# Block-sparse attention and a gated feed-forward in one kernel: mask rows by ScalarE, more zero products at the start, a spread mean product, V casts on VectorE, and a reordered end

## The chip, the cores and the metric

The kernel runs on one core of a Trainium2 chip. A core has five engines with a queue each: TensorE for matrix products (PE in the profile, with its weight loads as PEld), VectorE (DVE), ScalarE (ACT), GpSimd (POOL) and SyncE (SP), which here only issues DMAs. Each engine works through its instructions in order; they wait for one another by semaphores. The metric is the device time of one launch in microseconds (us). Before the change the median of three runs is 231.93 us, from 230.8 to 233.28.

## The reference

Attention over four batches of eight heads, 768 positions and 64 channels per head, with a mask made of blocks of 32, and then a feed-forward layer over the 3072 tokens of 512 channels:

```python
scores = scale * q @ k.T                 # per batch and head
# allowed: neighbouring blocks, first and last block row and column,
# and three sampled blocks for each block of queries
scores = np.where(mask, scores, -1e9)
attn = exp(scores - max) / sum
x = (attn @ v), heads side by side       # 3072 x 512

h = x @ w_in                             # 3072 x 1024
solu = h * softmax(h)
ln = (solu - mean) / sqrt(var + 1e-6) * g_ln
out = ln @ w_out                         # 3072 x 512
```

## The kernel before

**Tiling.** A batch is cut into three passes of 256 queries, so there are 12 passes. A pass has 12 units: four pairs of heads, three units for a pair, each unit 256 keys of both heads by 256 queries. A unit is four score products into a PSUM tile `sco` (two buffers), one exponential of 128x1024 on ScalarE (`exps`), and eight products of the exponentials with V (`outs`) into the tile `op` (one buffer). After the third unit of a pair VectorE normalises `op` into `xb`. The mask is part of the score product: below the 64 channels, `KT` and `QT` hold 24 more rows, block selectors for the keys and mask values for the queries.

**Feed-forward.** It runs one pass behind, in two layers of 128 tokens: `xb` is turned by a DMA into `xT`, eight products with `w_in` give `h` (`h_mms`, one PSUM buffer), ScalarE takes its exponential (`e_exp`), VectorE multiplies (`solu`) and takes statistics, a DMA turns `solu` into `lnT`, eight products with the centred weights `w_cen_sb` give `o` (`o_mms`), and VectorE scales and a DMA stores. The division by the softmax sum and by the standard deviation is folded into one factor, which GpSimd computes (`rstd`). The centred weights are prepared once: GpSimd multiplies `w_out` by `g_ln` (`prep_w`), TensorE takes its mean over the layer (`prep_mean`, eight products), VectorE copies the mean and subtracts it (`prep_cen`, eight times).

**Order.** Everything is unrolled and put in order by hand: `at(when, fn, ...)` files a step under a due time in units, `emit()` sorts by it, and what is emitted in this order is queued on its engine in this order. Unit 144 is the `end`. Steps before the plan (the mask, the first casts and turns, `scores(0)` and `scores(1)`) are emitted as they stand in the text. `zeros(n, pool)` issues n products of a zero tile (128x512) whose result nobody reads.

**The places the change touches.** The first mask rows of q: ScalarE copies them for head 0 from `m_ps` (line 599), VectorE copies head 0 to head 1 (line 604); ScalarE also brings the first turned q chunk to `QT` (line 602). `turn` of pairs 2 and 3 (lines 627 to 633). `prep_mean` at 19.0 and 19.6 and `prep_cen` from 19.9 (lines 684 to 688). `coming` (line 703), which files loads and casts of the next batch, the casts on GpSimd. The end: the list from line 880, with the last pass's layers (`x_last`, `h_end`, `ln_mm`, `ln_out`, `o_half`, `scale_half`), and `check_e` and `check_bad`, which test that all sums lie in a safe range. TensorE adds up the flags (`bad_ps`), VectorE writes them as an integer (`bad_i`), and lines 926 and 927 load it on every engine and branch around a slow general path that these inputs do not need.

## Time and profile before

| | |
|---|---|
| median of three runs | 231.93 us (230.8 to 233.28) |
| the profiled execution, its own time | 230.46 us |
| its span, first to last instruction | 228.5 us |
| TensorE busy | 210.6 us of the span |
| ScalarE busy | 174.0 us |
| VectorE busy | 154.2 us |
| GpSimd busy | 111.4 us |
| mean granted TensorE clock | 0.98 |

The page gives busy time by engine, then the span in 40 slices, the DMA queues, the chain of work that ended last, and the costliest groups of instructions. A busy share is an average over the whole span: stages with different limits are told apart by windows and by the timeline. A line of the timeline has the start in us, the duration in us, engine, line, operation, output and input tile, shapes and count, and in brackets the idle time of the engine just before it with what ended it. A row with several instructions has the time from the first one's start to the last one's end; matmuls overlap, so a row of several is shorter than the sum. A window row has the window, its length, the busy time (and number of instructions) of PE, PEld, DVE, ACT and POOL, then the granted TensorE clock, the DMA share and GB/s. The profiled execution's own time is 1.96 us above its span, and 1.47 us below the median.

### The profile page before, as it was taken

The numbers are of one execution on the slowest core, as the hardware profiler recorded it, in microseconds if no ns is written. First come the engines' busy times: TensorE is split into PE (matmuls) and PEld (weight loads), VectorE is DVE, ScalarE is ACT, GpSimd is POOL, SyncE is SP. The second block draws the span as 40 slices with busy tenths as digits, with TensorE's granted clock in tenths as the row PEclk, the third lists the DMA queues.
The fourth block names the chain that finished last, engine by engine and source line by source line (L and its number), as shares of the span: only waits on it lengthen the run. The fifth ranks groups of instructions, "written<-read, shape, count | busy, mean of one in ns | idle before, by whom it ended". The sixth has DMA issues, their size and how long they took to land.

```text
span 228.5 us, 5931 instructions
## 1 busy us (share of the span) xinstructions
PE 210.6 (92%) x2368; PEld 146.4 (64%) x2368; DVE 154.2 (68%) x352; ACT 174.0 (76%) x205; POOL 111.4 (49%) x155
## 2 busy tenths in 40 slices
PE   7896997999989999999999999999999999996970
PEld 2565864776756777776866777677676767663440
DVE  7876666877775765676775676667657655765860
ACT  4667885797786988797798898779789888783730
POOL 7999965247897325647825507739600000000010
PEclk9679999999999999999999999999999999999998
DMA  6999593339979449839749569489233458434021
GB/s 192 362 324 268 149 283 133 73 72 339 290 87 314 99 86 289 241 64 299 155 30 351 129 147 246 114 165 296 52 98 92 87 54 117 115 89 87 37 101 56
DMA packets 56148, 37.60 MB, mean 165 GB/s; under 512 B 38068, under 2 KB 51636, under 8 KB 56116
## 3 DMA queue, kind: packets, MB, share of 16 engines
q1 hardware_dynamic: 55172, 35.60, 61.5%
q0 software_dynamic: 528, 1.05, 2.4%
q10 hardware_dynamic: 416, 0.52, 0.8%
q8 instruction: 20, 0.33, 0.6%
q14 instruction: 12, 0.10, 0.1%
HBM read 23.07 MB, written 6.29 MB: 129 GB/s over the span
## 4 chain that ended last, share of the span: by engine, by line
PE 75%; DVE 9%; POOL 7%; DMA 3%; issue 2%; ACT 1%; DVEq 0%; POOLq 0%
PE sco L364 24%; PE o L481 14%; PE h L421 14%; PE op L388 14%; PE tp_k L329 2%; POOL KT L309 2%; POOL QT L309 2%; PE tp_q L329 2%; PE he L789 2%; DMA xT<-xb 1%; PE warm L556 1%; DVE xb L402 1%; DMA xTe<-xb 1%; DVE KT L309 1%; DVE w_cen_sb L673 1%
## 5 line engine op out<-in xcount | busy, mean ns | idle before, releaser
L375 ACT ACTIVATE exs<-sco 128x1024 bf16<-128x1024 f32 x144 | 141.6, 1025 | 16.5 <-PE sco L364 13.8
L364 PE MATMUL sco<-QT,KT 88*128 88x256 bf16 x576 | 88.6, 275 | 3.1 <-ACT exs L375 1.6
L364 PEld LDWEIGHTS <-KT 88*128 88x128 bf16 x576 | 55.5, 98 | 34.5 <-issue 7.2
L421 PE MATMUL h<-w_in_sb,xT 128*128 128x512 bf16 x176 | 55.2, 378 | 1.2 <-DVE solu L442 0.6
L388 PE MATMUL op<-VA,exs 128*128 128x65 bf16 x1152 | 52.0, 194 | 2.6 <-DVE xb L402 1.7
L388 PEld LDWEIGHTS <-exs 128*128 128x128 bf16 x1152 | 48.8, 97 | 6.0 <-issue 2.6
L474 POOL TENSOR_TENSOR rstd<-vpe,mhalf 128x1 f32<-128x1 f32 x24 | 13.2, 549 | 71.5 <-DVE vpe L472 64.6
L481 PE MATMUL o<-w_cen_sb,lnT 128*128 128x512 bf16 x176 | 45.1, 379 | 0.0
L430 ACT ACTIVATE e<-h 128x1024 bf16<-128x1024 f32 x22 | 22.5, 1023 | 20.5 <-PE h L421 19.1
L309 POOL COPY KT<-pt_k 64x768 bf16<-64x768 bf16 x24 | 19.7, 822 | 23.5 <-DVE pt_k L338 22.8
L401 DVE RECIPROCAL recip_all<-op 128x4 f32<-128x4 f32 x48 | 8.7, 181 | 30.6 <-PE op L388 30.3
L456 DVE BATCH_NORM_STATS2 stats<-solu 128x6 f32<-128x512 bf16 x46 | 29.3, 680 | 0.0
L442 DVE TENSOR_TENSOR solu<-h,e 128x1024 bf16<-128x1024 f32 x22 | 26.7, 1214 | 1.2 <-ACT e L430 1.2
L481 PEld LDWEIGHTS <-lnT 128*128 128x128 bf16 x176 | 15.8, 97 | 13.3
L492 DVE TENSOR_SCALAR ot<-o,rstd 128x512 f32<-128x512 f32 x20 | 15.0, 751 | 11.2 <-issue 6.3
L402 DVE TENSOR_TENSOR xb<-op,recip_all 128x256 bf16<-128x256 f32 x48 | 20.4, 424 | 1.7
L309 POOL COPY QT<-pt_q 64x768 bf16<-64x768 bf16 x24 | 19.7, 820 | 3.6 <-DVE pt_q L338 2.3
L421 PEld LDWEIGHTS <-xT 128*128 128x128 bf16 x176 | 15.5, 98 | 5.9 <-DMA xT<-xb 1.6
L309 POOL CAST qn<-st_q 128x768 bf16<-128x768 f32 (+2 forms) x19 | 14.4, 763 | 1.8 <-DMA st_q<-in_q_dram 1.5
L309 POOL CAST kn<-st_k 128x768 bf16<-128x768 f32 x15 | 12.7, 845 | 4.4 <-DMA st_k<-in_k_dram 2.9
L309 POOL CAST VA<-st_v 128x768 bf16<-128x768 f32 x16 | 13.1, 834 | 1.5 <-DMA st_v<-in_v_dram 1.3
L338 DVE COPY pt_q<-tp_q 128x768 bf16<-128x768 bf16 x12 | 6.7, 556 | 10.3 <-PE tp_q L329 10.3
(92 smaller groups left out, 151.5 us busy)
## 6 DMA issues: line engine op xcount, KB each, us to landing
st_v<-in_v_dram SPq DMA_DIRECT2D x16, 384.0 KB, 5.6
out_dram<-ot SPq DMA_DIRECT2D x23, 256.0 KB, 3.6
st_k<-in_k_dram SPq DMA_DIRECT2D x15, 384.0 KB, 4.6
st_q<-in_q_dram SPq DMA_DIRECT2D x12, 384.0 KB, 4.8
w_out_f<-in_moe_w_out_dram SPq DMA_DIRECT2D x4, 512.0 KB, 8.5
st_q<-in_q_dram SPq DMA_DIRECT2D x4, 256.0 KB, 6.9
w_in_sb<-in_moe_w_in_dram POOLq DMA_DIRECT2D x1, 1024.0 KB, 12.9
st_q<-in_q_dram SPq DMA_DIRECT2D x4, 128.0 KB, 4.3
```

The source lines that it names most:

```text
L309: eng.tensor_copy(out=o, in_=i)
L364: nc.tensor.matmul(sco[:, hh, kk * QW : (kk + 1) * QW], KT[b % 2][0:KR, h * NCH + 2 * u + kk, :], QT[b % 2][0:KR, h * NCH + PC * j : h * N ...
L375: nc.scalar.activation(out=exs_of[ps, pr][:, u].rearrange("p a b c -> p (a b c)"), in_=sco_of.pop(s).rearrange("p a b -> p (a b)"), func=A ...
L388: nc.tensor.matmul(op[:, hh, ic, :], exs[:, u, hh, kk, ic * TQ : (ic + 1) * TQ], VA[b % 2][:, 2 * pr + hh, 2 * u + kk, :], start=(u == 0 a ...
L402: nc.vector.tensor_tensor(out=xb_of[ps][:, :, 2 * pr * D : 2 * (pr + 1) * D].rearrange("p c (h d) -> p h c d", h=2), in0=op[:, :, :, 0:D], ...
L421: nc.tensor.matmul(h_of[ps, i][:, half, :], xT_of[ps][:, i * KD + c, :], w_in_sb[:, c, half * HF : (half + 1) * HF], start=(c == 0), stop= ...
L430: nc.scalar.activation(out=o, in_=h, func=ACT.Exp, scale=1.0, accum_out=esum_all[:, t : t + 1])
L442: nc.vector.tensor_mul(out=so, in0=h, in1=e)
L456: nc.vector.bn_stats(out=stat_of[ps, i][:, half, :], in_=so[:, half, :])
L474: nc.gpsimd.tensor_tensor(out=rstd_of[ps, i], in0=vpe, in1=mhalf, op=ALU.pow)
L481: nc.tensor.matmul(ops_of[ps, i], lnT_of[ps, i][:, c, :], w_cen_sb[:, c, :], start=(c == 0), stop=(c == KF - 1), skip_group_check=True)
L492: nc.vector.tensor_scalar(out=o, in0=i_, scalar1=r, scalar2=None, op0=ALU.mult)
```

## The change

Six edits. (1) ScalarE copies the first mask rows of q to both heads from PSUM, and VectorE brings the first turned q chunk to `QT`. (2) The zero products ahead of the first scores go into one tile: one more before the k turn, three in place of one after the q turn; after each of the units 0 to 3 three stand in place of two. The q turn of pair 3 is due one unit later. (3) The mean of `w_out` is taken two products at a time, at 19.85, 20.85, 21.85 and 22.85, and the eight subtractions are due from 23.1 on. (4) For batch 1, V of pairs 1 to 3 is cast by VectorE at fixed times, and the last V load is filed with the one before it. (5) At the end the order of the list is new: five products of the last but one pass's first layer come before the end, the last chunk of x is turned ahead of all products of the last pass's h, and these follow in one run; products of the older layers are regrouped. (6) The test is split: `check_e` early, the sum (`check_sum`) after the last factors, and `check_bad` last, behind both halves of the last output; the second half is scaled by ScalarE.

```diff
         def zeros(n, pool=p_o):
-            w = pool.tile([128, 512] if pool is not p_sco else [128, 2, 512], FP32,
-                          tag={p_o: "o", p_op: "op", p_sco: "sco"}[pool], name="warm")
-            w = w[:, 0, :] if pool is p_sco else w
+            w = pool
+            if pool in (p_o, p_op):
+                w = pool.tile([128, 512], FP32, tag="o" if pool is p_o else "op", name="warm")
...
-        row_q0 = rows(QT[0], 0, 1).rearrange("p o (i c) -> p (o i) c", i=2)
         mask_rows(nc.gpsimd, KT[0], 2)
         mask_rows(nc.vector, KT[0], 0)
+        warm_t = p_sco.tile([128, 2, 512], FP32, tag="sco", name="warm_t")[:, 0, :]
+        zeros(1, warm_t)
         turn_mm(0, 0, "k", p_op, 2, NCH)
-        zeros(1, p_sco)
+        zeros(1, warm_t)
         turn_out(0, 0, "k", DVE2, 0, 2)
-        nc.scalar.copy(out=row_q0, in_=m_ps[D:KR, :, 0 : S // 2])
+        for hh in range(2):
+            nc.scalar.copy(
+                out=rows(QT[0], hh, hh + 1).rearrange("p o (i c) -> p (o i) c", i=2),
+                in_=m_ps[D:KR, :, 0 : S // 2])
         turn_mm(0, 0, "q", p_o, 0, 2)
-        zeros(1, p_sco)
-        turn_out(0, 0, "q", (nc.scalar, nc.scalar), 0, 2)
+        zeros(3, warm_t)
+        turn_out(0, 0, "q", DVE2, 0, 2)
         turn_out(0, 0, "k", DVE2, 2, NCH)
-        nc.vector.tensor_copy(out=rows(QT[0], 1, 2), in_=rows(QT[0], 0, 1))
...
-            turn(w0 + 0.05, 0, pr, "q", p_o, 0, 2)
+            turn(w0 + (0.05 if pr == 2 else 1.0), 0, pr, "q", p_o, 0, 2)
...
         for n in range(4):
-            at(n + 0.9, zeros, 2, p_op)
+            at(n + 0.9, zeros, 3, p_op)
...
-            at(19.9 + 0.4 * c, prep_cen, c)
-        at(19.0, prep_mean, 0, 4)
-        at(19.6, prep_mean, 4, KF)
+            at(23.1 + 0.45 * c, prep_cen, c)
+        for n in range(4):
+            at(19.85 + n, prep_mean, 2 * n, 2 * n + 2)
...
-                at(t0 + 8.2 + 1.2 * n, cast, nc.gpsimd, b, pr, key)
+                if b == 1 and key == "v" and pr > 0:
+                    at((0, 38.6, 40.2, 43.2)[pr], cast, nc.vector, b, pr, key)
+                else:
+                    at(t0 + 8.2 + 1.2 * n, cast, nc.gpsimd, b, pr, key)
...
-                n_ld = [0, 0, 4, 0, 6, 1, 1]
+                n_ld = [0, 0, 4, 0, 6, 2, 0]
...
-        def scale_half(half, eng):
+        def scale_half(half, eng, q):
...
+            if eng is nc.scalar:
+                nc.scalar.activation(out=ot_of[LP, 1][:, m0:m1], in_=o2[half], func=ACT.Copy,
+                                     scale=rstd_of[LP, 1])
...
         def check_e():
-            check_r(n_r - 2 * PC, n_r)
             in_range(okr[:, n_r:], esum_all, 1e-6, 1e7)
+
+        def check_sum():
             nc.vector.reduce_sum(out=n_ok[:, 0:1], in_=okr, axis=AX.X)
```

The list at the end, as it stands after the change (`A` is ScalarE, `V` VectorE, `LP` the last pass):

```python
(o_mms, LP - 1, 0, 5, 8), (scaled, LP - 1, 0, A), (store, LP - 1, 0),
(x_last,), (h_end, 0, 0, KD - 1), (h_end, 0, KD - 1, KD),
(stats, LP - 1, 1), (rstd, LP - 1, 1), (check_r, n_r - 2 * PC, n_r),
(e_exp, LP, 0), (h_end, 1, 0, KD), (solu, LP, 0), (e_exp, LP, 1),
(o_mms, LP - 1, 1, 0, 3, tile_in(p_op, "op", "o_10")),
(ln_mm, 0), (ln_out, 0, A), (o_mms, LP - 1, 1, 3, 8), (solu, LP, 1),
(check_e,), (stats, LP, 0), (squares, 1), (ln_mm, 1), (ln_out, 1, V),
(o_mms, LP, 0, 0, 8, tile_in(p_sco, "sco", "oe0")), (mean_mms, 1),
(scaled, LP - 1, 1, A), (store, LP - 1, 1), (rstd, LP, 0), (rstd_sq, 1),
(check_sum,), (scaled, LP, 0, A), (store, LP, 0),
(o_half, 0, p_sco, "sco"), (o_half, 1, p_op, "op"),
(scale_half, 0, V, nc.sync), (scale_half, 1, A, nc.scalar), (check_bad,)
...
at(end - 1.15, o_mms, LP - 1, 0, 0, 5)    # before: at(end - 1.1, h_end, 0, 0, KD - 1)
```

Before, this list began with `o_mms` of five products, `x_last`, `stats`, two more `o_mms` and the last chunk of `h_end`; `check_e` and `check_bad` stood between the factors and the second `o_half`.

35 lines of the change are left out of this document (17 added, 18 removed).

## The prediction

> **What bounds the kernel now.** I read the page first (busy time, slices, chain of waits), then windows to tell the stages apart, then the timeline of those stages in which TensorE idles or runs slowly.
>
> ```profile
> PE 210.6 (92%) x2368; PEld 146.4 (64%) x2368; DVE 154.2 (68%) x352; ACT 174.0 (76%) x205; POOL 111.4 (49%) x155
> ...
> PEclk9679999999999999999999999999999999999998
> ...
> PE 75%; DVE 9%; POOL 7%; DMA 3%; issue 2%; ACT 1%; DVEq 0%; POOLq 0%
> ```
>
> TensorE is busy 92% of the span and carries 75% of the chain. The slices 1 and 2 (5.7 to 17 us) have a clock of 0.6 and 0.7. The windows show where there is room:
>
> ```profile
> 4.50:7.91 3.41, 2.40 (x16) 0.95 (x14) 3.24 (x7) 2.54 (x6) 3.28 (x4) 1.00 1.06 347
> 7.91:11.32 3.41, 3.24 (x19) 2.49 (x20) 2.61 (x7) 2.08 (x3) 3.36 (x6) 0.50 1.07 364
> 11.32:14.74 3.42, 3.42 (x18) 2.13 (x17) 2.14 (x3) 2.01 (x2) 3.01 (x4) 0.50 1.08 359
> 205.87:209.28 3.41, 1.65 (x22) 1.03 (x22) 2.02 (x5) 2.03 (x3) 0.55 (x1) 1.00 0.30 63
> ...
> 38.00:46.00 8.00, 6.24 (x83) 4.76 (x82) 7.21 (x18) 6.02 (x9) 1.99 (x3) 1.00 0.32 61
> 72.00:80.00 8.00, 8.00 (x97) 5.72 (x96) 4.97 (x12) 6.92 (x8) 4.13 (x6) 1.00 0.59 175
> ```
>
> From 7.91 to 14.74 TensorE has half the clock and is busy all the time: there it is the bound because it is slow. From 72 on it is busy without a gap, and nothing in the change removes work there. From 38 to 46 it idles 1.76 of 8 us while VectorE is nearly full. So four places can give time: the start, the mean and its subtraction, the wait for V, and the end. Everything between follows the start of its stage, so a microsecond won early is carried along.
>
> **Part 1, the start.** The first score products wait for the mask row that VectorE copies last:
>
> ```profile
> 5.63 0.79 ACT L599 CAST QT<-m_ps 24x768 bf16<-24x768 f32 x1
> 5.64 1.50 DVE L309 COPY KT<-tp_k 64x256 bf16<-64x256 bf16 x4
> 7.16 0.86 DVE L604 COPY QT<-QT 24x768 bf16<-24x768 bf16 x1
> 8.08 0.61 PE L364 MATMUL sco<-QT,KT 88*128 88x256 bf16 x2 [0.84 <-DVE QT L604]
> 8.72 1.02 ACT L375 ACTIVATE exs<-sco 128x1024 bf16<-128x1024 f32 x1 [1.52 <-PE sco L364]
> ```
>
> After the change ScalarE makes both row copies, 5.63 + 0.79 + 0.79 = 7.21. VectorE brings two k pieces, then two of q, about 0.3 each, to 7.0. The five zero products there are hidden behind these copies. Scores start at 7.28 instead of 8.08, the first exponential at 7.9 instead of 8.72: 0.8 won. The larger share is the clock.
>
> ```profile
> 12.75 1.06 PE L556 MATMUL warm<-zer 128*128 128x512 bf16 x2
> 15.04 0.60 PE L556 MATMUL warm<-zer 128*128 128x512 bf16 x2
> 12.14 1.08 DVE L590 COPY QT<-QT 24x1536 bf16<-24x1536 bf16 x1
> 14.48 1.14 DVE L309 COPY KT<-tp_k 64x768 bf16<-64x768 bf16 x2 [1.26 <-PE tp_k L329]
> 15.23 2.86 ACT L375 ACTIVATE exs<-sco 128x1024 bf16<-128x1024 f32 x3 [1.22 <-PE sco L364]
> 18.95 0.59 DVE L309 COPY QT<-tp_q 64x256 bf16<-64x256 bf16 x2
> 20.36 0.66 PE L388 MATMUL op<-VA,exs 128*128 128x65 bf16 x16 [1.34 <-DVE xb L402]
> 21.56 1.94 ACT L375 ACTIVATE exs<-sco 128x1024 bf16<-128x1024 f32 x2 [1.25 <-PE sco L364]
> ```
>
> The clock changes 3.41 us apart, at 4.50, 7.91 and 14.74; it fell after a window with TensorE busy 2.40, some of it transposes, and it held at the end of the window at 205.87 with 1.65 and no transposes. The first of these windows gets three more zero products, some 0.65 at full clock, and the scores 0.8 earlier; I therefore take it that the clock holds. Then VectorE sets the pace: from 7.0 it has two more k pieces, the mask rows and the turned k and q of pairs 1 and 2. Walked with these rows (up to 1.08 for mask rows, 1.14 for a pair's k, 0.59 for its q) it brings pair 2 at 14.25, and the seventh exponential starts at 14.9; it is the third of the three at 15.23, so at 17.1 before (15.23 + 2.86 - 1.02): 2.2 won. The four zero products in the units 0 to 3 cost nothing, as TensorE has slack at full clock; with the clock still down they cost 0.43 each. The q turn of pair 3, one unit later, takes 0.59 of copies from in front of the normalisation for which TensorE waited 1.34 at 20.36. Together the tenth exponential, at 21.56 before, comes at 19.1 to 19.4. I take 2.4; bounds 0.6 (clock down) and 2.8.
>
> **Part 2, mean and centring.**
>
> ```profile
> 33.98 1.89 PE L667 MATMUL mean_ps<-w_out_sb,mean_w 128*128 128x512 bf16 x8
> 37.07 1.02 ACT L430 ACTIVATE e<-h 128x1024 bf16<-128x1024 f32 x1 [2.30 <-PE h L421]
> 39.15 0.60 PE L364 MATMUL sco<-QT,KT 88*128 88x256 bf16 x4 [1.43 <-ACT exs L375]
> 40.35 0.61 PE L421 MATMUL h<-w_in_sb,xT 128*128 128x512 bf16 x2 [0.61 <-DVE solu L442]
> ...
> L673 DVE TENSOR_TENSOR w_cen_sb<-w_out_sb,mean_sb x8: 407/416/1037, 36.7 to 42.7; 128x512 bf16<-128x512 bf16 x8
> ```
>
> Eight mean products in a row held back scores and h; ScalarE idled 2.30, and TensorE then idled 1.43 behind it and 0.61 behind VectorE: 2.04 in all. Two products a unit are 0.45 us each time, which the exponentials (1.02 a unit) can bear, so the 1.43 go. But the eight subtractions now fall due in four units, 22.85 to 26.85, which last 4 x 1.33 = 5.3 us (from 72 to 80 ScalarE's 6.92 are six exponentials of a unit and a layer's, so six units in 8 us). VectorE then has 8 x 0.45 = 3.6 of subtractions, some 0.7 for the mean copy (estimated from the 0.69 of `lnTe`, quoted in part 4), and 4.97 / 8 x 5.3 = 3.3 of usual work: 7.6 in 5.3, so it runs up to 2.3 late. Before it had the same extra work in a stretch no longer, and TensorE lost 0.61 by it; I leave that loss and 0.1 more in, and take 1.3 won; bounds 0 and 2.0.
>
> **Part 3, V by VectorE.**
>
> ```profile
> 68.03 0.66 PE L388 MATMUL op<-VA,exs 128*128 128x65 bf16 x16 [0.88 <-POOL VA L309]
> ...
> L309 POOL CAST VA<-st_v x16: 822/826/916, 10.9 to 158.8; 128x768 bf16<-128x768 f32 x16
> ```
>
> GpSimd is full before this point, and TensorE waits 0.88 for a V cast. Off GpSimd the cast is due two units earlier than its use, and the wait goes. VectorE's price for 768 fp32 elements is not in the trace: between 0.57 (half of the 1.14 for two copies of 768 bf16 elements) and 0.83 (GpSimd's own); I take 0.8, three times, within the 4.6 units (6.1 us) from 38.6 to 43.2, of which 3.03 / 8, or 2.3, are free by the window from 72. Won: 0.9, bounds 0 and 1.2.
>
> **Part 4, the end.**
>
> ```profile
> 207.07 1.01 ACT L375 ACTIVATE exs<-sco 128x1024 bf16<-128x1024 f32 x1
> 208.28 1.47 PE L789 MATMUL he<-w_in_sb,xTe 128*128 128x512 bf16 x6 [1.76 <-DMA xTe<-xb]
> 209.58 0.41 PE L388 MATMUL op<-VA,exs 128*128 128x65 bf16 x8
> 211.57 2.33 PE L789 MATMUL he<-w_in_sb,xTe 128*128 128x512 bf16 x10
> 212.22 1.02 ACT L430 ACTIVATE e<-he 128x1024 bf16<-128x1024 f32 x1 [4.13 <-PE he L789]
> 218.49 0.69 DVE L309 COPY lnTe<-ln_tp 128x1024 bf16<-128x1024 bf16 x1 [0.98 <-PE ln_tp L799]
> 221.84 0.19 PE L875 MATMUL bad_ps<-ones_c,bad 128*1 128x1 f32 x2 [1.36 <-DVE bad L870]
> 222.07 0.15 DVE L876 CAST bad_i<-bad_ps 1x1 int32<-1x1 f32 x1 [0.37 <-PE bad_ps L875]
> 223.57 0.37 ACTq L497 DMA_DIRECT2D out_dram<-ot_last  x1
> ...
> L927 PEldq COMPARE_BRANCH  x1: 3738/3738/3738, 222.9 to 222.9; - x1
> ...
> out_dram<-ot_last ACTq DMA_DIRECT2D x1, 128.0 KB, 3.0
> ```
>
> The last exponential ends at 208.08, but its products with V stand behind six h products that wait for a DMA, and start at 209.58. Five o products (0.22 each, as ten h products take 2.33 with the last one's tail) now fill that wait, and `outs` starts at 208.15. The last x is ready 1.4 earlier; then come two transposes and all eight h products, 1.75, ahead of the exponential, which starts at 211.35 instead of 212.22: 0.87. The next exponential gains the same. The turn of the second layer no longer stands behind ten o products, so the idle 0.98 ahead of its copy `lnTe` goes too, less some 0.5 (an estimate) for the range test that now stands there: 1.36 won, ending at 217.82 instead of 219.18. From there to the last store's issue it was 4.39; without TensorE's wait for the test between the two halves, 1.36, it is 3.03: 220.85 instead of 223.57, 2.7 won.
>
> But the test comes last. Its integer needs `bad_ps` behind the second half: TensorE is done about 0.5 ahead of that store, at 220.3, and 0.2 later the integer is written, at 220.5 instead of 222.22: only 1.7 earlier. Before, two things end together: the store at 223.57 + 3.0 = 226.57, and TensorE's branch, 222.9 + 3.74 = 226.6; the span ends 1.9 later. The branch waits for the integer, so with its 3.74 the tail wins 1.7 and not 2.7. [...] The measurement decides, and I take 1.7; bounds 1.2 and 2.7.
>
> **Sum.** 2.4 + 1.3 + 0.9 + 1.7 = 6.3. The profiled execution took 230.46 (span 228.5 and 1.96 around it), so 224.2 for one like it. The median of before lies 1.47 higher, with runs up to 233.28. I take half of that for the new median, 0.7, and predict 224.9, 7.0 under the median.
>
> **Rivals.**
>
> (a) The clock falls all the same at the end of its first full window. Against it: the added products. For it: they are zeros and short, and nothing shown says what level is needed between 1.65 and 2.40. The start then wins 0.6, the time is 226.7.
>
> (b) VectorE becomes the bound in parts 2 and 3, so that what TensorE no longer waits for the mean and for V it waits for normalisation and `solu`. For it: 7.21 busy of 8 us from 38 to 46. Against it: only three casts and no more subtractions than before. Parts 2 and 3 then win nothing: 227.1.
>
> [...]
>
> (d) Slower: GpSimd holds VectorE up. The subtractions took 0.41 to 1.04, the longest while GpSimd cast. If all take 1.04, VectorE has 4.7 more in part 2, which then loses 3.4; if each V cast also stands through one of GpSimd's (0.83), three are 4.9 on VectorE with 2.3 free, and part 3 loses 2.6. With 2.4 and 1.7 won elsewhere that is 1.9 lost, 232.4, or 233.1 with the 0.7. It decides from a loss of 4.1 in parts 2 and 3 on. [...]
>
> **How the numbers follow.** My forecast 0.46, (a) 0.15, (b) 0.19, (c) 0.15, (d) 0.05. Low end: (c) together with part 2 at its bound, 224.9 - 1.0 - 0.7 = 223.2, and without the 0.7 added for the median 222.5. High end: (b) with half of the 1.8 that (a) costs, 228.0, and the part of the median's 1.47 that I left out brings 228.3. Within 1%, about what a measurement here tells from no change, means above 229.6; that needs (a) and (b) together with a slow draw, 0.07. Slower by over 1% (234.3) is the far part of (d), 0.03. Faster: 0.90.
>
> **What would show it.** Right: clock 1.00 from 4.5 to 20; first scores waiting for ScalarE or VectorE near 7.3; the mean products in four rows of two and no idle of 1.4 behind them; no wait for V near 64; `bad_i` the last on VectorE, and TensorE's branch of some 3.7 us ending over 1 us after the last store has landed. Wrong: a clock of 0.5 after 7.9 (a); waits of TensorE for `xb`, `solu` or `w_cen_sb` of more than 1.5 us in sum (b), with subtractions near 1 us (d); a branch of a few tenths (c).

## The result and the profile after

The changed kernel takes 228.83 us (median; 226.98 to 233.97) where the kernel before took 231.91 in runs on the same chip: a ratio of 0.987, 95% interval 0.985 to 0.990. It is faster by 3.1 us; 7.0 were forecast, and 228.83 lies above the top of the range, 228.3. The sign was right and the size less than half. Three sets of times are compared below: medians of whole runs, ratios to the kernel before with their intervals, and stages of single traces. The ratios, and the mean granted clocks given beside them, leave out the slow runs of each kernel, over 1.5% above its fastest.

The profiled execution of the changed kernel took 228.12 us, its span is 226.1. From its page the busy times, the granted clock in 40 slices and the chain of waits by engine:

```profile
PE 208.3 (92%) x2336; PEld 146.3 (65%) x2375; DVE 156.7 (69%) x355; ACT 174.9 (77%) x205; POOL 109.9 (49%) x152
...
PEclk9999999999999999999999999999999999999996
...
PE 74%; DVE 13%; DMA 4%; ACT 3%; issue 2%; POOL 1%; SPq 0%; DVEq 0%; POOLq 0%; ACTq 0%
```

The 6 and 7 at the start of the clock line are gone. But the chain has changed too: VectorE carries 13% of it (9% before) and DMA, which carried 3%, 4%. Some of TensorE's waits have become waits for these two. The windows of the same execution (columns as before: start and end, length, busy time of each engine, granted clock, DMA share, GB/s):

```profile
38.00:46.00 8.00, 7.55 (x95) 5.77 (x96) 6.63 (x16) 5.90 (x7) 3.13 (x5) 1.00 0.37 67
72.00:80.00 8.00, 7.84 (x92) 5.63 (x93) 5.23 (x13) 6.83 (x9) 3.56 (x6) 1.00 0.50 148
...
44.00:48.00 4.00, 2.62 (x39) 1.93 (x39) 3.93 (x12) 3.10 (x5) 3.09 (x4) 1.00 0.34 66
```

From 38 to 46 TensorE now works 7.55 us instead of 6.24. The idle time has moved to 44 to 48: TensorE 2.62 of 4, VectorE 3.93 of 4. The same window of the kernel before had none:

```profile
44.00:48.00 4.00, 4.00 (x49) 2.74 (x47) 2.89 (x8) 3.05 (x5) 3.56 (x5) 1.00 0.34 66
```

To set the traces beside one another, exponentials are counted from 0 (the rows of `exs` on ScalarE); exponential k starts unit k. The table has four stretches in us: the start of unit 18, from there to unit 33 (the mean's stretch), unit 39 to 45 (where V was waited for), and from exponential 143 to the end of the span. Between 45 and 143 all of them take 133.0 to 133.4. The last two columns have the time from which the trace's record of the granted clock has it full, and the stretches in which it then has half. Ahead of the first record, at 7.42 and 8.24, a zero product of the changed kernel took 0.61 and 0.63 us, and behind it, at 13.58, 0.38.

| kernel | start of 18 | 18 to 33 | 39 to 45 | 143 to end | first full clock | then lowered |
|---|---|---|---|---|---|---|
| before | 31.53 | 23.80 | 9.65 | 21.4 | 4.5 | 7.9 to 14.7 |
| changed | 31.89 | 24.08 | 9.40 | 18.8 | 10.5 | not before the end |
| changed_again | 31.24 | 24.08 | 10.53 | 18.8 | 5.8 | 19.5 to 22.9 |
| start_alone | 30.60 | 24.25 | 9.66 | 21.1 | 7.2 | not before the end |
| v_alone | 31.23 | 25.22 | 9.23 | 20.8 | 6.8 | 20.4 to 23.8, 40.9 to 44.3 |
| end_alone | 31.82 | 23.91 | 9.66 | 19.5 | 5.9 | 19.6 to 23.0 |
| v_cast_only | 31.83 | 25.36 | 9.14 | 21.0 | 6.6 | 20.3 to 23.7, 40.7 to 44.2 |
| mean alone (label old_start) | 32.12 | 24.08 | 9.66 | 20.9 | 5.0 | 8.4 to 11.8, 22.1 to 25.5 |
| fill_dips | 31.14 | 23.63 | 9.66 | 20.8 | 5.1 | 8.5 to 11.9 |
| start_undone | 31.79 | 24.08 | 10.08 | 18.8 | 5.7 | 19.3 to 22.7 |
| mean_early | 30.15 | 24.44 | 10.47 | 18.8 | 4.3 | not before the end |
| late_load | 29.90 | 24.08 | 9.12 | 18.7 | 4.3 | not before the end |
| late_check | 30.26 | 24.07 | 9.31 | 18.2 | 4.5 | not before the end |
| after_no_zeros | 30.89 | 24.08 | 10.17 | 18.7 | 7.2 | not before the end |
| early_check | 30.54 | 24.08 | 12.28 | 18.0 | 6.0 | 67.4 to 70.8 |
| best | 31.55 | 24.43 | 9.33 | 18.1 | 7.0 | not before the end |
| cen_after_q | 30.57 | 24.18 | 9.18 | 18.0 | 5.8 | not before the end |

Read by columns, the end won more than forecast, the mean's stretch nothing, the V stretch little or less than nothing, and the start depends on the last two columns. From unit 18 to 45 the stretches that a lowered clock falls into are the longest of their columns: 18 to 33 in v_alone and v_cast_only (25.22 and 25.36, the others 23.63 to 24.44), 39 to 45 in early_check (12.28, the others 9.12 to 10.53).

### The profile page after: what moved, and what is told of

The parts are those of the page before. It is cut to its first block, busy times and chain, and to the rows that moved or that the text cites. A ratio compares the mean times of both kernels' runs of the same rounds, so it can differ in the third digit from the quotient of the medians.

```text
span 226.1 us, 5902 instructions
## 1 busy us (share of the span) xinstructions
PE 208.3 (92%) x2336; PEld 146.3 (65%) x2375; DVE 156.7 (69%) x355; ACT 174.9 (77%) x205; POOL 109.9 (49%) x152
## 4 chain that ended last, share of the span: by engine, by line
PE 74%; DVE 13%; DMA 4%; ACT 3%; issue 2%; POOL 1%; SPq 0%; DVEq 0%; POOLq 0%; ACTq 0%
PE sco L364 24%; PE o L481 14%; PE op L388 14%; PE h L421 14%; DMA xT<-xb 4%; PE tp_q L329 2%; PE tp_k L329 2%; DVE KT L309 1%; DVE w_cen_sb L676 1%; DVE xb L402 1%; ACT exs L375 1%; ACT e L430 1%; DVE stats L456 1%; PE warm_t L556 1%; DVE QT L309 1%
## 5 line engine op out<-in xcount | busy, mean ns | idle before, releaser
L364 PE MATMUL sco<-QT,KT 88*128 88x256 bf16 x576 | 86.9, 272 | 2.2 <-ACT exs L375 1.4
L421 PE MATMUL h<-w_in_sb,xT 128*128 128x512 bf16 x153 | 49.4, 378 | 2.3 <-DMA xT<-xb 1.4
L481 PE MATMUL o<-w_cen_sb,lnT 128*128 128x512 bf16 x162 | 43.5, 379 | 2.2 <-DVE pt_q L338 1.4
L430 ACT ACTIVATE e<-h 128x1024 bf16<-128x1024 f32 x22 | 22.5, 1024 | 19.2 <-PE h L421 14.9
L309 POOL COPY KT<-pt_k 64x768 bf16<-64x768 bf16 x24 | 20.1, 836 | 22.3 <-DVE pt_k L338 21.6
L402 DVE TENSOR_TENSOR xb<-op,recip_all 128x256 bf16<-128x256 f32 x48 | 20.4, 425 | 1.7
L309 POOL CAST VA<-st_v 128x768 bf16<-128x768 f32 x13 | 10.9, 853 | 1.9 <-DMA st_v<-in_v_dram 1.8
```

Source lines behind the costliest of these rows:

```text
L309: eng.tensor_copy(out=o, in_=i)
L364: nc.tensor.matmul(sco[:, hh, kk * QW : (kk + 1) * QW], KT[b % 2][0:KR, h * NCH + 2 * u + kk, :], QT[b % 2][0:KR, h * NCH + PC * j : h * N ...
L402: nc.vector.tensor_tensor(out=xb_of[ps][:, :, 2 * pr * D : 2 * (pr + 1) * D].rearrange("p c (h d) -> p h c d", h=2), in0=op[:, :, :, 0:D], ...
L421: nc.tensor.matmul(h_of[ps, i][:, half, :], xT_of[ps][:, i * KD + c, :], w_in_sb[:, c, half * HF : (half + 1) * HF], start=(c == 0), stop= ...
L430: nc.scalar.activation(out=o, in_=h, func=ACT.Exp, scale=1.0, accum_out=esum_all[:, t : t + 1])
L481: nc.tensor.matmul(ops_of[ps, i], lnT_of[ps, i][:, c, :], w_cen_sb[:, c, :], start=(c == 0), stop=(c == KF - 1), skip_group_check=True)
```

## Experiments

**The four parts, each alone.** Each kernel is the one before with one part of the change's diff: the start (`mask_rows` to `turn`, with the zero products), the mean, V's cast and load, or the end. The core line or two of each:

```diff
# start_alone
-        nc.scalar.copy(out=row_q0, in_=m_ps[D:KR, :, 0 : S // 2])
+        for hh in range(2):
+            nc.scalar.copy(
...
-            at(n + 0.9, zeros, 2, p_op)
+            at(n + 0.9, zeros, 3, p_op)
# mean_alone
-        at(19.0, prep_mean, 0, 4)
-        at(19.6, prep_mean, 4, KF)
+        for n in range(4):
+            at(19.85 + n, prep_mean, 2 * n, 2 * n + 2)
# v_alone
+                if b == 1 and key == "v" and pr > 0:
+                    at((0, 38.6, 40.2, 43.2)[pr], cast, nc.vector, b, pr, key)
...
-                n_ld = [0, 0, 4, 0, 6, 1, 1]
+                n_ld = [0, 0, 4, 0, 6, 2, 0]
# end_alone
-            (o_mms, LP - 1, 0, 0, 5),
+            (o_mms, LP - 1, 0, 5, 8),
...
```

> The kernel before with the start alone changed (mask rows by ScalarE, zero products, the later q turn of pair 3). Theory A, from the two traces: the start is worth little on average, 0.3 to 1.0 us over the runs, because what starts the first scores is a mask chain ahead of the edit (it ended at 5.03 us in the one trace and at 6.57 in the other), and because the zero products only help where the clock would otherwise have fallen. Theory B, the prediction: 2.4 us faster.

> The kernel before with the mean product and the subtractions alone moved. Theory A: no gain or up to 0.5 us slower; the four pairs of mean products win 1.2 to 1.4 us by the exponential of unit 24, and TensorE then loses 1.2 to 1.6 us in one wait ahead of the first o products, with VectorE still subtracting. Theory B, the prediction: 1.3 us faster.

> The kernel before with the V casts of batch 1 on VectorE and the last V load earlier, alone. Theory A: 0 to 0.4 us faster; TensorE's wait of 0.9 for a V cast goes, and a wait for the turned x of 0.5 to 0.8 us comes in its place about one us earlier, as the earlier V load shares the DMA with that turn. Theory B, the prediction: 0.9 us faster and no new wait.

> The kernel before with the end alone changed. Theory A: 2.4 to 2.8 us faster, nearly all that the whole change wins; TensorE's branch ends the run, with some 3.5 us from 221.4 on, and what follows it is 1.2 us and not 1.9. Theory B, the prediction: 1.7 us faster with 1.9 behind the branch.

Measured: start 231.31, ratio 0.998 (0.994 to 1.003); mean 231.44, 0.995 (0.991 to 0.999); V 231.65, 1.001 (0.997 to 1.005); end 230.39, 0.994 (0.989 to 0.999); the kernel before took 232.50. By their ratios the end won 1.4 us, below the 2.4 to 2.8 expected, and the mean 1.2, near the 1.3 of the forecast and against theory A; the mean's repeat (old_start, below) won 0.3 with an interval that reaches no change. The intervals of the start and of V include no change. The trace of mean_alone comes from an execution with a mean granted clock of 0.961 (span 233.9) and is not used. So it isn't one part that fell short: the start and V did, and the mean's traces, shown below, hold no gain in its stretch.

The start alone shows why a part can be right in a trace and small in the times. Its traced execution had a mean granted clock of 0.996, while the other nine runs compared had 0.971 to 0.984, about the 0.978 of the kernel before: the trace is the exception. Rows of the timeline of v_alone, which has the old start, in an execution where the clock is full from 6.8 to 20.4 (start, duration, operation, and in brackets the idle time before it and what ended it):

```profile
14.69 1.02 ACT L375 ACTIVATE exs<-sco 128x1024 bf16<-128x1024 f32 x1 [0.30 <-PE sco L364]
14.82 1.85 DVE L590 COPY QT<-QT 24x1536 bf16<-24x1536 bf16 x1
...
19.23 0.66 PE L388 MATMUL op<-VA,exs 128*128 128x65 bf16 x16 [2.50 <-DVE xb L402]
20.43 2.10 ACT L375 ACTIVATE exs<-sco 128x1024 bf16<-128x1024 f32 x2 [2.41 <-PE sco L364]
```

And the window of this trace before the clock falls:

```profile
17.00:20.40 3.40, 1.17 (x28) 1.15 (x29) 1.98 (x6) 1.02 (x2) 3.29 (x6) 1.00 1.09 275
```

The row at 14.69 is the seventh exponential. My walk gave 14.9 for the new start and 17.1 for the old one, read from one execution in which the clock fell at 7.9. Where it does not fall there, the old start is as early as the new one. Then both wait for VectorE: here a mask copy of 1.85 us and the normalisation (`xb`), for which TensorE idles 2.50. In the window ahead of 20.4 TensorE is busy 1.17 of 3.40 us, and there the clock falls instead.

**fill_dips.** Is it the clock? The kernel before gets 16 zero products in three places where TensorE idles (units 6.8, 21.8 and 142.9) and no other change but a pool that `zeros` may use.

```diff
+        at(6.805, zeros, 6, p_h)
+        at(21.795, zeros, 5, p_o)
+        at(end - 1.105, zeros, 5, p_o)
```

> The kernel before plus 16 zero products in the three waits in which TensorE is least busy: six ahead of the products that wait for the first normalised x (unit 6.8), five ahead of the scores of unit 21.8, five ahead of the h products at the end that wait for a DMA. Nothing else is changed. Theory C, the clock: the clock falls for 3.4 us after a window of 3.4 us in which TensorE is busy about 1.6 us or less, and where the windows lie differs from run to run; filling the dips raises the mean granted clock of the runs from 0.978 to 0.984 or more and wins 0.6 to 1.5 us. Theory D, the clock is not what the change wins by: mean clock within 0.002 of before, and time the same or up to 0.5 us longer by the added products.

Measured: 229.54 against 231.95, ratio 0.988 (0.985 to 0.992); the mean granted clock of the runs compared is 0.987, that of the kernel before 0.978. Sixteen products that compute nothing are worth 2.4 us of medians, more than the 0.6 to 1.5 expected and most of what the whole change brings. Its trace has a single lowered window, 8.5 to 11.9. The products take away no work, and the clock of the runs rose with them, by 0.009. The changed kernel's runs have 0.989, nearly the same rise. So a good part of what can be won in these places goes with the clock, which the forecast priced at the start alone. Which of the three places wins it, and how much of the changed kernel's 3.1 us it is, was not split.

**after_no_zeros.** The changed kernel with the zero products of the kernel before, so with the new order alone.

```diff
-            at(n + 0.9, zeros, 3, p_op)
+            at(n + 0.9, zeros, 2, p_op)
```

> The changed kernel with as many zero products as the kernel before: one and one instead of one, one and three at the start, two after each of the units 0 to 3. Theory C: mean granted clock of the runs below that of the changed kernel (0.989), 0.980 to 0.986, and 0.5 to 1.3 us longer than it, so 1.8 to 2.6 us faster than before. Theory D: the same as the changed kernel, 3.0 us faster than before.

Measured: 229.75, ratio 0.988 (0.982 to 0.994), and a trace with full clock from 7.2 on. The clock held without the added products in this execution, with a mean of 0.992. But the mean over the runs compared is 0.981, within theory C's 0.980 to 0.986, where the changed kernel has 0.989. So the trace is again better than most runs, and the products seem to hold the clock up. What that is worth in time isn't shown: the ratio is the changed kernel's, and its interval is wide.

**v_cast_only.** V's three casts on VectorE, but the load of V in its old unit.

> The kernel before with the V casts of batch 1 on VectorE, the last V load left where it was. Theory A (the wait for the turned x in the run with the load moved comes from that load): no wait of TensorE for the turned x near unit 40, or at most 0.3 us, and 0.5 to 0.9 us less from unit 39 to unit 45 than the 9.65 us before; the time 0.3 to 0.9 us less than before. Rival (the wait comes from VectorE's casts): the same wait of 0.5 us or more, and no gain.

Measured: 231.44, ratio 0.997 (0.992 to 1.002). In the table units 39 to 45 take 9.14 instead of 9.65: the cast wins 0.5 there, for 0.9 forecast. With the load moved up as well the stretch takes 9.23 to 10.53 in v_alone, changed, changed_again, start_undone and mean_early. That turned my attention to the load, which the forecast had not costed.

**early_check.** The changed kernel with the test's sum on ScalarE and its compare on GpSimd, and the integer written ahead of the last two scalings.

```diff
-            nc.vector.reduce_sum(out=n_ok[:, 0:1], in_=okr, axis=AX.X)
-            nc.vector.tensor_scalar(out=bad, in0=n_ok[:, 0:1], scalar1=float(n_r + n_e),
...
+            nc.scalar.activation(out=okj, in_=okr, func=ACT.Square, accum_out=n_ok[:, 0:1])
+            nc.gpsimd.tensor_scalar(out=bad, in0=n_ok[:, 0:1], scalar1=float(n_r + n_e),
...
```

> The changed kernel with the test's integer ahead of the last products: ScalarE sums the flags behind the squares, GpSimd compares, and the product for the integer stands ahead of both halves. Theory A (TensorE's branch of 3.5 us alone sets the end, the stores land some 2.7 us earlier): the integer is ready near 219.3 instead of 220.5, the branch ends 1.0 to 1.5 us earlier, and the run is 1.0 to 1.5 us shorter than the changed kernel, 4.0 to 4.5 faster than before. Rival: something else behind the stores sets the end, and the time is that of the changed kernel, within 0.4.

Measured: 228.33, ratio 0.981 (0.977 to 0.986). From exponential 143 to the end it takes 18.0 instead of 18.8, although the branch itself became longer (4.18 for 3.54). That is less than the 1.0 to 1.5 expected; the part on the end below shows why. The branch was still on the way to the end, as the forecast had it. In the same trace units 39 to 45 took 12.28, with the load of V moved up as in the changed kernel and, from 67.4 on, a lowered clock.

**mean_early.** The changed kernel with the mean and the subtractions one unit earlier, to find room on VectorE.

```diff
-            at(23.1 + 0.45 * c, prep_cen, c)
+            at(22.1 + 0.45 * c, prep_cen, c)
...
-            at(19.85 + n, prep_mean, 2 * n, 2 * n + 2)
+            at(18.85 + n, prep_mean, 2 * n, 2 * n + 2)
```

> The changed kernel with the mean products and the eight subtractions one unit earlier (18.85 + n and 22.1 + 0.45 c instead of 19.85 + n and 23.1 + 0.45 c); nothing is left out. In the changed kernel's trace VectorE is full from 44 to 48 us and TensorE waits 1.37 us for it ahead of the products of the first layer's output, which gives back the 1.2 to 1.3 us that the spread mean products had won. Theory (VectorE is the bound behind the mean, its place in time is what matters): the subtractions lie where VectorE has room, the wait of 1.37 shrinks below 0.5, unit 33 starts some 23.2 us behind unit 18 instead of 24.1, and the time is 0.5 to 1 us under the changed kernel's 228.8. Rival (the extra 3.6 us of VectorE work must be paid for wherever they stand, since VectorE has no room before 44 either): the wait only moves ahead, 24 us from unit 18 to 33, time within 0.3 us of 228.8.

Measured: 227.91, ratio 0.989 (0.983 to 0.994), no different from the changed kernel. The wait did not shrink (1.60 instead of 1.37, ended by the same copy), and units 18 to 33 took 24.44. The theory fell; the rival, that VectorE has no room before 44 either, held.

**late_load.** The changed kernel with the load of V in its old unit.

```diff
-                n_ld = [0, 0, 4, 0, 6, 2, 0]
+                n_ld = [0, 0, 4, 0, 6, 1, 1]
```

> The changed kernel with the second early V load back in its old unit (n_ld of the second batch [0, 0, 4, 0, 6, 1, 1] as before the change), the three V casts staying on VectorE; nothing is left out. Theory (the early load holds up the transposing DMA of xT, which sets the new wait of TensorE at 63 to 68 us): no wait for that DMA above 0.3 us, 9.1 to 9.2 us from unit 39 to unit 45 instead of 9.4 (and 10.2 and 12.3 in two other kernels with the early load), no lowered clock at 67, time 0.2 to 1 us under the changed kernel's. Rival (the transposing DMA is late by itself, whatever else loads): the wait of 0.5 us or more is there again, 9.4 us or more, the same time.

Measured: 227.78, ratio 0.986 (0.982 to 0.990); units 39 to 45 take 9.12 as expected, and the wait for `xT` that was to stay below 0.3 is 0.40. The lower median fits, but the interval overlaps that of the changed kernel.

**A run that held the wrong kernel.** The label old_start stands over the kernel before with the mean's edit alone, by a mistake in putting it together. Its expectation speaks of a kernel that did not run.

> The changed kernel with the start of the kernel before (one ScalarE copy of a mask row and one by VectorE, ScalarE turning q, fewer zero products, q of pair 3 turned a unit earlier); parts 2 to 4 as changed; nothing is left out. By the forecast's step the start is worth 2.4 us: 231.2. By the theory of the runs so far VectorE's chain sets unit 9 at 20.4 to 20.7 us with both starts when the clock holds, and the start is worth only the windows of lowered clock that its zero products and its order avoid: 0 to 1 us above the changed kernel's 228.8, with a mean clock 0.003 to 0.01 lower, and unit 5 at 13.4 us (if the first windows are warm) instead of 14.1 to 14.6.

Measured: 231.13, ratio 0.999 (0.995 to 1.002). It counts as a repeat of mean_alone: the two together put part 2 at 0.3 to 1.2 us by their ratios, while units 18 to 33 take 24.08 against 23.80 before. The question was asked again by start_undone.

**best.** The changed kernel with early_check, late_load, mean_early and six zero products at unit 6.8 together.

> The changed kernel with four edits: the test's sum by ScalarE and its compare by GpSimd with the integer written ahead of the last two scalings (as in early_check), the V load in its old unit, the mean one unit earlier, and six zero products at unit 6.8. Nothing is left out. If each is worth what it is held to be worth (0.7 for the test, 0.2 to 0.7 for the load, 0.5 to 1 for the mean, 0 to 0.5 for the clock): 226.5 to 227.5 us, ratio to the kernel before 0.977 to 0.981, mean clock 0.99 or more. If the mean and the load are worth nothing: as early_check, 228.1.

Measured: 227.21, ratio 0.984 (0.980 to 0.988), and the highest mean clock of all, 0.997. The ratio missed the 0.977 to 0.981 that the parts would have added up to: unit 18 starts at 31.55, 1.65 us behind late_load, and units 18 to 33 take 24.43. Its clock came up at 7.0 where late_load's came up at 4.3, so it isn't shown whether the six products or the draw cost the start.

**changed_again, start_undone and late_check,** on one chip. start_undone is the changed kernel without its start, late_check the changed kernel with late_load and early_check, whose edits stand above.

> The changed kernel itself, beside the two others of this call on one chip. Expected as before: 228 to 229 us, ratio to the kernel before 0.985 to 0.99; 9.4 us or more from unit 39 to 45; no lowered clock between 7 and 60 us wherever its windows happen to lie.

> The changed kernel with the start of the kernel before (one ScalarE copy of a mask row and one by VectorE, ScalarE turning q, fewer zero products, q of pair 3 turned a unit earlier); parts 2 to 4 as changed; nothing is left out. By the forecast's step the start is worth 2.4 us. By the traces so far, unit 18 starts 1.0 us later with the old start on average (31.1 to 32.1 us in six profiles with the old start, 29.9 to 31.9 in seven with the new one), always behind a window of lowered clock either near 8 us (clock first up before 5.2 us) or near 20 us (first up later): 0.7 to 1.3 us above changed_again. Rival (the start is worth nothing by itself, start_alone's 0.5 being noise): within 0.3 us of changed_again, and no lowered window.

> The changed kernel with the V load in its old unit (as late_load) and the test's sum by ScalarE, its compare by GpSimd and the integer written ahead of the last two scalings (as early_check); nothing is left out. If the load costs 0.5 us or more and the test 0.5 to 0.7 and they add: 226.7 to 227.3 us, 1.2 to 2 us under changed_again, 9.1 to 9.2 us from unit 39 to 45, 17.9 us from the start of exponential 143 to the end instead of 18.8. If the load's gain was the draw of another chip: 227.8 to 228.2.

Measured: 227.96, 228.56 and 226.04, ratios to the kernel before 0.984 (0.979 to 0.989), 0.987 (0.982 to 0.991) and 0.978 (0.973 to 0.982). By these medians the start is worth 0.6 us beside the other parts, a little under the 0.7 expected, and the two intervals overlap; the mean granted clock is 0.982 without it and 0.992 with it. late_check beats both kernels: 1.9 us under the changed one on the same chip, and below its own expectation. One expectation missed: in changed_again the clock did fall, at 19.5. The windows of its trace between the changes of the clock show behind what:

```profile
12.69:16.11 3.42, 3.42 (x44) 2.56 (x42) 3.28 (x6) 3.07 (x3) 3.20 (x5) 1.00 1.14 340
16.11:19.52 3.41, 1.44 (x32) 1.16 (x31) 3.10 (x7) 1.94 (x2) 3.35 (x9) 1.00 1.08 243
19.52:22.94 3.42, 3.42 (x40) 2.60 (x37) 0.61 (x2) 2.05 (x2) 3.34 (x3) 0.51 1.08 260
```

TensorE was busy 1.44 of 3.41 us, and the next window has half the clock. So the new start makes the fall rarer beside the other parts, but doesn't exclude it: it fell before 60 us in all seven traces of the table with the old start, and in one of ten with the new one. The low clocks of the other runs of start_alone and after_no_zeros say that ten traces are too few for a rate.

**cen_after_q.** late_check with the last four subtractions behind VectorE's copy of q. The copy frees the PSUM buffer that the first layer's products need. It changes VectorE's order and no amount of work.

```diff
-            at(23.1 + 0.45 * c, prep_cen, c)
+            at(23.1 + 0.45 * c if c < 4 else 25.93 + 0.01 * c, prep_cen, c)
```

> late_check with one more edit: the last four of the eight subtractions are put behind VectorE's copy of q (pt_q), which frees the PSUM buffer that the products of the first layer's output need; the same work, nothing is left out. In all kernels with the mean spread, TensorE waited 1.3 to 1.6 us for that copy. Theory (order, not amount): the copy ends 1.6 us earlier, the products start about 1 us earlier and then run as fast as the subtractions come (0.41 each against 0.22 a product), units 18 to 33 take 23.0 to 23.5 us instead of 24.07, and the time is 0.5 to 1 us under late_check's 226.04: 225.0 to 225.5. Rival (amount: VectorE's backlog is paid by TensorE wherever it stands): the wait moves to the subtractions or to solu behind them, 23.9 us or more, 226 us.

Measured: 226.25, ratio 0.977 (0.971 to 0.983), the same as late_check. First the timeline of the changed kernel in this stretch:

```profile
38.21 0.60 PE L364 MATMUL sco<-QT,KT 88*128 88x256 bf16 x4 [0.99 <-ACT exs L375]
...
40.46 0.59 PE L670 MATMUL mean_ps<-w_out_sb,mean_w 128*128 128x512 bf16 x2
...
44.61 2.05 DVE L676 TENSOR_TENSOR w_cen_sb<-w_out_sb,mean_sb 128x512 bf16<-128x512 bf16 x4
...
46.59 0.55 DVE L338 COPY pt_q<-tp_q 128x768 bf16<-128x768 bf16 x1
...
47.18 1.67 PE L481 MATMUL o<-w_cen_sb,lnT 128*128 128x512 bf16 x6 [1.37 <-DVE pt_q L338]
```

Four subtractions stand ahead of the copy `pt_q`, and TensorE waits 1.37 for it. The same stretch of cen_after_q's timeline:

```profile
43.62 0.56 DVE L338 COPY pt_q<-tp_q 128x768 bf16<-128x768 bf16 x1
44.10 2.20 DVE L676 TENSOR_TENSOR w_cen_sb<-w_out_sb,mean_sb 128x512 bf16<-128x512 bf16 x4
...
44.33 1.67 PE L481 MATMUL o<-w_cen_sb,lnT 128*128 128x512 bf16 x7
...
46.77 1.21 DVE L442 TENSOR_TENSOR solu<-h,e 128x1024 bf16<-128x1024 f32 x1
...
48.12 0.59 PE L421 MATMUL h<-w_in_sb,xT 128*128 128x512 bf16 x2 [1.39 <-DVE solu L442]
```

The copy comes first and the products start without a wait. Then the next h products wait 1.39 for `solu`, which now stands behind the subtractions. The same 1.4 us has changed its name, and units 18 to 33 take 24.18. So it is the amount of VectorE's work and not its order, as far as two other orders (this one and mean_early) can show it; no run takes work off VectorE there.

## Why the forecast was right and wrong

**Part 1, the start: 2.4 forecast, 0.4 to 0.6 measured, neither clear of nothing.** The mechanism was right where the trace is like the one that I read. In late_load, with the clock full from 4.3 on as in the profile of before, the rows are these:

```profile
5.62 1.48 ACT L601 CAST QT<-m_ps 24x768 bf16<-24x768 f32 x2 [0.21 <-PE m_ps L578]
...
7.79 4.10 ACT L375 ACTIVATE exs<-sco 128x1024 bf16<-128x1024 f32 x4 [0.68 <-PE sco L364]
...
12.40 3.20 ACT L375 ACTIVATE exs<-sco 128x1024 bf16<-128x1024 f32 x3 [0.51 <-PE sco L364]
...
14.50 1.90 DVE L590 COPY QT<-QT 24x1536 bf16<-24x1536 bf16 x1
...
18.36 0.66 PE L388 MATMUL op<-VA,exs 128*128 128x65 bf16 x16 [1.74 <-DVE xb L402]
...
19.56 1.94 ACT L375 ACTIVATE exs<-sco 128x1024 bf16<-128x1024 f32 x2 [1.76 <-PE sco L364]
```

The first exponential starts at 7.79 (forecast 7.9), the seventh is the third of the row at 12.40 and starts near 14.6 (14.9), the tenth at 19.56 (19.1 to 19.4; the mask copy took 1.90 where I had put 1.08, and TensorE waited 1.74 for `xb`). The failing step is the subtraction: "17.1 before" and "at 21.56 before" were taken as what the old start costs, though they were one draw of the clock. In the table the old start's clock falls near 8 us when it first came up by 5.1, and near 20 when later. Traces whose clock first came up at a like time show it, with fill_dips and best left out. Where it came up by 5.1, the tenth exponential starts at 21.1 to 21.6 with the old start and at 19.6 to 19.8 with the new one. Where it came up between 5.6 and 7.3, it starts at 20.4 to 21.3 and at 20.5 to 20.7. On average unit 18 starts at 31.7 with the old start (six traces) and at 30.7 with the new one (nine), 1.0 us apart. The changed kernel's own profile shows another side: its first exponential started at 10.98, and unit 18 was no earlier than before. That is a draw too, and of something else. The row that makes the mask, in the profile of before and in that of the changed kernel:

```profile
4.21 0.81 DVE L569 SCALAR_TENSOR_TENSOR mask_l<-acc,stat_m 24x24 bf16<-24x24 f32 x1
```

```profile
5.16 1.41 DVE L569 SCALAR_TENSOR_TENSOR mask_l<-acc,stat_m 24x24 bf16<-24x24 f32 x1
```

The mask, which no edit touches and the first scores need, was ready at 6.57 instead of 5.02. The cast of the sampled blocks ahead of it began at 2.71 instead of 2.36. So 1.5 us of the late start are this chain; for the rest the clock, which came up only at 10.5, is the likely cause. The 0.4 to 0.6 left in the times are below that 1.0. A part of the rest is taken back where `xT` is waited for (part 3): of the kernels with the V load moved up, early_check left out, six reach unit 39 between 63.5 and 65.3, 1.9 us apart, and unit 45 between 73.9 and 74.8, 0.9 apart.

Rival (a), that the clock falls at the end of its first full window, came true in none of the ten traces with the new start; it fell later in one of them, at 19.5. In the table the clock first came up anywhere from 4.3 to 10.5 us, so the places of its steps differ from run to run.

**Part 2, the mean: 1.3 forecast, nothing in its stretch.** The products came in four pairs as forecast, and the idle time behind them fell from 1.43 to 0.99, where the forecast had it go. The step that failed is "I leave that loss and 0.1 more in": I had worked out that VectorE would run up to 2.3 us late and charged TensorE 0.7 for it. The 2.3 was nearer. From unit 18 to 24 the changed kernel wins 1.65 us (8.32 instead of 9.97), and from there to unit 33 it loses 1.9, of which 1.37 is the wait ahead of the first layer's products; cen_after_q shows that the loss follows VectorE's amount of work. This is rival (b), to which I had given 0.19, in this part. Why the mean alone is then 0.3 to 1.2 us faster by its ratios isn't shown by its own two traces, as lowered clocks elsewhere disturb them. The others suggest the clock again. A window of v_alone, which has the old mean:

```profile
37.50:40.90 3.40, 1.63 (x15) 1.03 (x15) 3.37 (x9) 3.13 (x5) 0.02 (x1) 1.00 0.01 2
```

Behind it the clock fell, at 40.9, and in v_cast_only at 40.7; there units 18 to 33 took 25.2 and 25.4. That is two of the five traces that have the old mean and no zero products added to it; in the eleven of the table with the spread mean the clock never fell between 25 and 60. So spreading the mean can win about 1.3 us (25.3 less 24.0) in those executions in which the clock falls there, which would fit the times; these are few traces.

**Part 3, V: 0.9 forecast, 0.5 for the cast and a loss for the load.** The casts cost about what was bounded (two of them 0.55 and 0.56 us, one 0.86, for bounds of 0.57 and 0.83), and the wait for GpSimd is gone. From the changed kernel, the group of the casts (min/median/max in ns), and from its timeline the wait in the old one's place:

```profile
L309 DVE CAST VA<-st_v x3: 553/558/862, 64.2 to 72.0; 128x768 bf16<-128x768 f32 x3
```

```profile
67.52 0.60 PE L421 MATMUL h<-w_in_sb,xT 128*128 128x512 bf16 x2 [0.78 <-DMA xT<-xb]
```

The failed step is an omission. The changed line of `n_ld` loads one V six units earlier, and part 3 gave that load no price and named no queue. It stands on SP's queue in front of the transposing DMA of `xT`. From the timeline of changed_again, SP's rows and the wait behind them:

```profile
58.18 0.54 SPq L300 DMA_DIRECT2D st_v<-in_v_dram  x1
...
59.34 0.38 SPq L300 DMA_DIRECT2D st_v<-in_v_dram  x1
60.52 1.41 SPq L413 DMA_TRANSPOSE xT<-xb  x1
...
68.00 0.60 PE L421 MATMUL h<-w_in_sb,xT 128*128 128x512 bf16 x2 [1.92 <-DMA xT<-xb]
```

In late_load the load at 59.34 isn't there, and the same products wait:

```profile
65.14 0.60 PE L421 MATMUL h<-w_in_sb,xT 128*128 128x512 bf16 x2 [0.40 <-DMA xT<-xb]
```

The turned x lands 6.3 us behind its issue in the changed kernel and 7.4 in changed_again. Whether the load holds it up on the queue or on the DMA engines was not told apart. Taking the load back gives 9.12 us from unit 39 to 45 instead of 9.40 and 10.53. In changed_again and mean_early, which came to unit 39 by 64.2, the wait was 1.9; in the changed kernel and v_alone, which came at 64.9 and 65.3, it was 0.8 and 0.6. So this wait also takes back time won earlier.

**Part 4, the end: 1.7 forecast, 1.4 alone by the ratio and 2.6 between the two traces.** The steps are found where the forecast had them. The timeline of the changed kernel, and the rows of its branch line:

```profile
208.40 0.43 PE L388 MATMUL op<-VA,exs 128*128 128x65 bf16 x8 [0.17 <-ACT exs L375]
...
211.61 1.02 ACT L430 ACTIVATE e<-he 128x1024 bf16<-128x1024 f32 x1 [1.36 <-DVE mv L466]
...
217.13 0.67 DVE L309 COPY lnTe<-ln_tp 128x1024 bf16<-128x1024 bf16 x1
...
219.99 0.19 PE L886 MATMUL bad_ps<-ones_c,bad 128*1 128x1 f32 x2
...
220.34 0.14 DVE L887 CAST bad_i<-bad_ps 1x1 int32<-1x1 f32 x1
220.45 0.33 SPq L497 DMA_DIRECT2D out_dram<-ot_last  x1
220.65 0.37 ACTq L497 DMA_DIRECT2D out_dram<-ot_last  x1
```

```profile
L938 PEldq COMPARE_BRANCH  x1: 3538/3538/3538, 221.4 to 221.4; - x1
```

`outs` at 208.40 (forecast 208.15), the exponential at 211.61 (211.35), `lnTe` done at 217.80 (217.82), the last store issued at 220.65 (220.85), the integer written at 220.48 (220.5), and a branch of 3.54 that ends at 224.91, 2.4 us behind the landing of that store (its 128 KB took 1.9). The 0.15 given to (c), and the 1.0 in the low end, take the store for what ends the run; no run shows that, here the branch does. What I had not foreseen is that the span ends 1.23 behind the branch, and not 1.88 as in the profile of before. In late_check, early_check and cen_after_q, which also have the V casts on VectorE, it ends 1.2 to 1.3 behind it. It doesn't look like the end's doing: end_alone, without these casts, takes 19.5 from exponential 143, and the six kernels of the table with the same end and the casts (changed, changed_again, start_undone, mean_early, late_load, after_no_zeros) take 18.7 to 18.8. So 0.65 us of the 2.6 (1.88 less 1.23) seem to go with part 3's edit; by what isn't shown.

In late_check the integer comes earlier still (the compare on GpSimd, the integer, the two stores):

```profile
215.60 0.25 POOL L882 TENSOR_SCALAR bad<-n_ok 128x1 f32<-128x1 f32 x1 [4.85 <-ACT okj L881]
...
217.38 0.14 DVE L888 CAST bad_i<-bad_ps 1x1 int32<-1x1 f32 x1
...
218.64 0.33 SPq L497 DMA_DIRECT2D out_dram<-ot_last  x1
219.11 0.37 ACTq L497 DMA_DIRECT2D out_dram<-ot_last  x1
```

```profile
L939 PEldq COMPARE_BRANCH  x1: 4378/4378/4378, 218.2 to 218.2; - x1
```

The integer is there 11.9 us behind the start of exponential 143 (217.52 - 205.58) instead of 13.1, so 1.2 earlier. The branch, longer here, ends only 0.6 earlier (16.95 us behind that start instead of 17.58), at 222.53 beside the last store, which lands at 222.5 (219.11 and the 3.4 of its landing). The tie of the kernel before is back, and the end wins 0.6. In both traces the two end within 0.1 us of each other (226.59 and 226.57 before), and the store, issued 0.7 (before) and 1.0 us (late_check) behind the start of the branch, lands 3.0 and 3.4 behind its issue; in the changed kernel it is issued 0.7 ahead of the branch and lands 1.9 behind its issue. Whether one of them waits for the other isn't shown, but by these numbers the store and the branch can't be priced apart when they overlap.

**The sum.** By the stages of traces: start 1.0 where the profiles are averaged, mean -0.1 (24.08 for 24.0, the mean of before, start_alone and end_alone), V +0.25 or -0.9, end 2.3 (21.1, the mean of before, start_alone, v_alone and v_cast_only, less 18.8; what ends the span behind the branch is in it). That makes 2.3 to 3.5, and 3.1 were measured; what a steadier clock wins outside these traces is not in it. The 0.7 put on for the median came out by luck: the changed kernel's median lies 0.7 over its profiled execution, which is one draw. The top of the range was added up wrongly: 228.0 and the 0.77 of the median's 1.47 that was left out make 228.8, not 228.3. The measured 228.83 lies at that edge too, since parts 1 to 3 all fell short at once. Rival (d), VectorE held up by GpSimd, shows in single rows only: in the changed kernel the longest subtraction took 1.04 and the other seven near 0.41.

## What to carry to other kernels

When an engine's backlog has been worked out and a later stage needs that engine, charge the whole backlog to the bound engine until some idle time that takes it up has been found. Price every line of a diff, a moved DMA first of all: here TensorE waited 1.92 us (changed_again) for the next transfer behind it on the queue, and 0.40 without it (late_load). And a stage read from one execution whose clock changed in it is one draw: look for a second execution, compare its mean clock with those of the other runs, or walk both kernels with the same clock, before the difference is called a gain.

## What the runs showed of the hardware

The granted clock changed 3.41 us apart or at a multiple of that: at 4.50, 7.91, 14.74 and 226.37 in the profile of before, at 10.53 and 222.16 in the changed kernel's. Behind steps of that length in which TensorE had been busy 0.91 us (end_alone, up to 19.6), 1.17 and 1.63 (v_alone, rows above) and 1.44 (changed_again, rows above) it fell. Behind 1.65 (before, 205.87 to 209.28), 1.85 (start_alone, 17.4 to 20.8), and 1.99 and 2.25 (changed, 44.65 to 48.06 and 17.35 to 20.77) it held. But at the start it fell behind 2.40 (before, 4.50 to 7.91), so the busy time alone doesn't tell the two apart. In the profile of before it came back at 14.74 with TensorE busy 3.24 and 3.42 us in the two steps at half clock. What decides, and why the start differs, stays open.

A copy of 24 x 1536 elements by VectorE took 0.55 us from 8.04 on in late_load. A GpSimd cast that began 0.06 later took 1.18, where the cast of the same shape at 6.98 took 0.82: 0.36 more, while the copy had 0.49 still to run. From 14.50 on, beside a DMA issue of GpSimd (0.97 from 14.02) and a cast (0.84 from 15.00), the same copy took 1.90, longer than either of them, and it ended 0.56 behind the cast (16.40 and 15.84). In v_alone, beside the same two (1.07 from 14.07, 0.84 from 15.15), it took 1.85. So in each of these places one of the two engines' instructions was longer than elsewhere; by what isn't shown.

The branch of TensorE took 3.54 us in the changed kernel, 3.74 before, 4.18 in early_check and cen_after_q, and 4.38 in late_check; in the changed kernel those of the four other engines took 0.05 to 0.07. What sets its length isn't shown.
